# Four engines in order of emission in a two-layer attention, with deferred work and a later plan for the output projections

## The chip, the cores and the metric

The kernel runs on one core of a Trainium2 chip. The core has five engines with a queue each: TensorE (PE in the profile, its weight loads as PEld), VectorE (DVE), ScalarE (ACT), GpSimd (POOL) and SyncE (SP), which here only issues transfers. The metric is the device time of one execution in microseconds (us), smaller being better.

## What is computed

The reference applies the same two blocks twice, attention A and then a gated MLP B, to 2048 rows of 640 numbers. Cut to what matters:

```python
def A(x):                                  # 32 heads of 20, 4 segments of 512 rows
    q, k, v = x @ wq, x @ wk, x @ wv       # by head
    M = z = 0
    for s in range(4):
        logits = qs @ ks.T * scale + causal_mask
        a_dot = softmax(logits) @ vs
        pq = phi(qs)                       # phi(t) = t + 1 if t > 0 else exp(t)
        a_mem = (pq @ M) / (pq @ z + 1e-6)
        outs += [g * a_mem + (1 - g) * a_dot]
        M, z = M + phi(ks).T @ vs, z + sum(phi(ks))
    return concat(outs) @ wo

def B(x):
    z = gelu(x @ w_in)                     # halves z1, z2 of 864
    gate = w_sp @ layernorm(z2) + b_sp     # 2048 x 2048, over the rows
    return (z1 * gate) @ w_out

for layer in range(2):
    x = x + A(layernorm(x))
    x = x + B(layernorm(x))
```

Products are made in float16 halves: a number is split into a high part and the rest (`..h`, `..l`), and a product is three matmuls, high by high, high by low and low by high.

## The kernel before

Each layer has three phases. Phase 1a is the attention, phase 1b the remaining output projections and the first product of B, phase 2 the product with `w_sp` and the second product. The change is in phase 1a (and in two helpers that it calls).

**Steps.** The heads of a segment are taken in 16 pairs, so there are 64 pairs in a layer. A pair is scored in 3 steps, 192 in all, 48 in a segment. In a step (`scores`, L713) PE makes a part of two products: `es`, the logits of pair n with keys on partitions, and `mp`, those of pair n + 2 with queries on partitions, for the row maxima. Each has one bank pair of PSUM. ACT then takes the exponential of `es` into `P` (L747), and DVE reduces `mp` to `mx` (L754: 1024 columns in the first step of three, 768 and 256 in the second, 512 in the third). The finished maxima of a pair are transposed by PE (`maxes`, L773, `mtp`), split by ACT and DVE into `mr` (L775, L776), and written by SP into four rows of the query tile `qs`, so that the next score product subtracts them. `cast` (L764, L765) splits `P` into `PH` on ACT and `PL` on POOL. `pvs` (L795) is the product with the values, `combine` (L799) divides (`rs`, `ab` on DVE), adds on POOL, and after the last pair of a group of heads (a unit, five in a segment) splits the result `oat` into `ohl` and stores it.

**Dense work between steps.** The rest of the attention's products are spread between the steps. `unit` (L600) makes the queries and keys of a unit of heads: 15 matmuls each into `qps` and `kps`, the split into `qhl` and `khl` (L217, L218), and the feature map phi: `eq` (an exponential on ACT, L621, and a product on DVE, L622), then `phq` or `phk` on DVE (L624). Keys are split again into `phl` (L629, L630) and transposed by a transfer into `pkh`, `pkl` (L633). `update` (L666) adds a unit's phi(k) by v to the memory: PE into `mup` (L676, L678), DVE into `mst` (L680). `read` (L637) reads the memory: PE into `num`, DVE `den` and `gm` (L660 to L663). `value` (L551) makes the values of 128 rows in two products `vps`, evicted by ACT and DVE into `vs` (L567, L568). `project` (L578) makes the output projection of 128 rows in two products `yps`, added to the input by DVE (L592, L596); `load_o` (L571) fetches its input ahead of time. `prep` (L540) loads, normalises, splits and transposes 128 rows of input for the products; `split_t` (L202) has the cast `xnhl` (L205). All dense products share two PSUM banks (tag `dn`); `mtp`, `mup` and a part of `num` share one (tag `ms`).

**What sets the order.** `phase1a` (L943) puts PE alone under a hand-written order (`manual_schedule`): PE's instructions stand as the code emits them, step by step. The instructions of the other engines are put in order by the framework's scheduler, from its own estimate of the times. `run` (L825) emits: before step 0, `early` makes the first four blocks of values and the first unit; then in each step the fetch of a pair, its scores, the maxima, the value products, the casts, and up to the step's end what four streams have due: `fills` (loads of inputs ahead of their use), `background` (weights of the next phases: reductions for their scales, L52 and L58, and splits), `dense`, and `reads`. The dense stream follows `plan` (L857), one string for a segment: a digit is a unit of that segment (0 the first one of the next), `v` a block of values and `p` an output projection. Each string is spread evenly over 48 steps, LEAD = 14 steps ahead of the segment. 12 of the 16 projections (`NWO`) are made here; phase 1b does the last four. Phase 1b also splits the first half of `w_in` (`wi0h`, L72, and `wi0l`, L73); the scheduler is free to put such instructions of ACT, DVE and POOL among those of the attention, where buffers allow.

```python
        ctx.enter_context(g.tc.manual_schedule(engines={mybir.EngineType.PE}))
        ...
        plan = ["1v2v3v4v0", "1234vvvv0pp", "1p2p3v4vv0vp", "1p2p3p4pppp"]
```

Of the kernel before, what the change touches and what calls it, by code (L numbers as in the profile page):

```python
# [8 lines left out]
F32 = mybir.dt.float32  # L9
F32R = mybir.dt.float32r  # L10
F16 = mybir.dt.float16
# [64 lines left out]
class Weight:  # L76
# [12 lines left out]
    def load(self, stage, width=864, tag="wst"):  # L89
# [4 lines left out]
        if self.made:  # L94
            for t, d in ((self.h, self.kept[0]), (self.l, self.kept[1])):
                nc.sync.dma_start(t[:, :full], d[:, :full])
                if rest:
                    nc.sync.dma_start(t[:rest, full], d[:rest, full])
                yield
            return  # L100
        for k in range(self.nk):
            n = 128 if k < full else rest
            for c in range(0, self.cols, width):
# [3 lines left out]
                split_scaled(self.g, self.h[:n, k, c:c + w], self.l[:n, k, c:c + w], st, self.c)  # L107
                yield
        for t, d in ((self.h, self.kept[0]), (self.l, self.kept[1])):
# [57 lines left out]
def other_scales(g, stage, pool, psum, tag):  # L167

    nc = g.nc
    for i, w in enumerate((g.wo, *g.wi, g.wu)):  # L170
        width = D if w.cols == D else w.cols // 2
        j = 0
        for k in range(w.nk):
            n = min(128, w.dram.shape[0] - 128 * k)
            for c in range(0, w.cols, width):
                t = stage.tile([128, D], F32, tag="bg", name="wmst")[:n, :width]
                nc.sync.dma_start(t, w.dram[k * 128:k * 128 + n, w.c0 + c:w.c0 + c + width])
                nc.vector.tensor_reduce(g.wap[:n, i, j:j + 1], t, AX.X, ALU.max, apply_absolute_value=True)
                j += 1
                yield  # L180
# [6 lines left out]
def layernorm(g, xt, out, d, nch, mult=1.0):  # L187
# [11 lines left out]
    nc.vector.tensor_scalar(out, xt, mv[:, 0:1], rs, ALU.subtract, ALU.mult)  # L199
# [290 lines left out]

class Attention:
# [9 lines left out]
    def __init__(self, g, x, o_d, x1_d):  # L501
# [7 lines left out]
        self.mem, self.last = None, -1  # L509
# [30 lines left out]
    def prep(self, t):  # L540
        g, nc = self.g, self.nc
# [3 lines left out]
        xn = self.e1.tile([128, D], F32, tag="xn", name="xn")  # L545
        layernorm(g, xt, xn, D, 2, XS)
        xh, xl = self.xt[s % 2]
        hl = self.e1.tile([128, 2, D], F16, tag="xh", name="xnhl")
        split_t(g, hl[:, 0], hl[:, 1], xh[:, :, c], xl[:, :, c], xn, low=nc.gpsimd)

    def value(self, t):  # L551
# [4 lines left out]
        for n in range(2):  # L556
# [8 lines left out]
            v = self.vs[s % 2][:, t % 4, n * 16:(n + 1) * 16, :]  # L565
            ps = ps.rearrange("p (h d) -> p h d", d=DH)
            nc.scalar.mul(v[:, :, 0:DH], ps, QS)  # L567
            nc.vector.scalar_tensor_tensor(v[:, :, DH + 1:], ps, QS, v[:, :, 0:DH], ALU.mult, ALU.subtract)  # L568
# [9 lines left out]
    def project(self, t):  # L578
# [7 lines left out]
        for n in range(2):  # L586
# [9 lines left out]
            nc.vector.scalar_tensor_tensor(x1[:, c], ps, g.yw, xt[:, c], ALU.mult, ALU.add)  # L596
        nc.sync.dma_start(self.x1_d[t], x1)


    def unit(self, s, m):  # L600
# [3 lines left out]
        for nm in ("q", "k"):  # L604
            if nm == "k" and self.mem is not None:
                yield from self.update(*self.mem)
# [9 lines left out]
            hl = self.u2.tile([128, 2, L], F16, tag="hl", name=f"{nm}hl")  # L616
            split_psum(g, hl[:, 0], hl[:, 1], ps, QS)
            self.stack(nm, s, m, hl)
            if (nm == "q" and s > 0) or (nm == "k" and s < NSEG - 1):
                e = self.u2.tile([128, L], F32, tag="tmp", name="eq")  # L620
                nc.scalar.activation(e, ps, AF.Exp, scale=g.rq if nm == "q" else g.rk)  # L621
                nc.vector.tensor_scalar(e, e, 1.0, g.gq if nm == "q" else g.gk, ALU.min, ALU.mult)  # L622
                ph = (self.u4 if nm == "q" else self.u1).tile([128, L], F32, tag=f"ph{nm}", name=f"ph{nm}")
                nc.vector.scalar_tensor_tensor(ph, ps, 0.0, e, ALU.max, ALU.add)  # L624
                if nm == "q":
                    self.phq[m] = ph
                else:
                    hl = self.u2.tile([128, 2, L], F16, tag="hl", name="phl")
                    nc.scalar.mul(hl[:, 0], ph, g.sig)  # L629
                    nc.vector.scalar_tensor_tensor(hl[:, 1], ph, g.sig, hl[:, 0], ALU.mult, ALU.subtract)  # L630
                    self.pk = [self.u1.tile([128, 4, 128], F16, tag="pk" + p, name="pk" + p) for p in "hl"]
                    for i, o in enumerate(self.pk):
                        nc.sync.dma_start(o, hl[:, i], transpose=True)  # L633
        if s < NSEG - 1:
            self.mem = (s, m)

    def read(self, s, m):  # L637
# [7 lines left out]
        for c0 in range(0, nh, 6):  # L645
# [3 lines left out]
            p, tag = (self.pm, "ms") if c0 else (self.pd, "dn")  # L649
            tp = p.tile([128, L], F32, tag=tag, name="num")[:, :4 * n * (DH + 1)].rearrange("p (t h d) -> p t h d", t=4, h=n)  # L650
            for t in range(4):
# [3 lines left out]
                if low:  # L655
# [3 lines left out]
            den = self.u2.tile([128, 4, 6], F32, tag="den", name="den")[:, :, :n]  # L659
            nc.vector.scalar_tensor_tensor(den, tp[:, :, :, DH], g.epsd, g.gate[:, heads[c0]:heads[c0] + n].unsqueeze(1).to_broadcast((128, 4, n)),  # L660
                                           ALU.add, ALU.mult)
            nc.vector.reciprocal(den, den)
            nc.vector.tensor_tensor(gm[:, :, c0:c0 + n, :], tp[:, :, :, 0:DH],  # L663
                                    den.unsqueeze(3).to_broadcast((128, 4, n, DH)), ALU.mult)

    def update(self, s, m):  # L666

        g, nc = self.g, self.nc
        self.mem = None
# [10 lines left out]
        nc.vector.tensor_tensor(new, mp, g.bmask[:, m, :n].unsqueeze(2).to_broadcast((128, n, DH + 1)), ALU.mult)  # L680
        if s > 0:
            nc.gpsimd.tensor_tensor(new, new, old, ALU.add)
# [327 lines left out]
```

## Time and profile before

| | us |
|---|---|
| median of 3 runs | 2587.47 |
| lowest and highest of them | 2585.75, 2590.23 |
| the profiled execution | 2581.99 |
| its span | 2580.3 |
| first layer: attention from the first value product to the last value product by P | 31.9 to 752.6 |
| second layer: the same | 1318 to 2007.8 |

Over the span the engines are busy as follows (us, share of the span, instructions):

```profile
PE 2276.9 (88%) x21706; PEld 1360.2 (53%) x21706; DVE 1505.0 (58%) x2806; ACT 1154.7 (45%) x1398; POOL 899.5 (35%) x713
```

Two kinds of numbers are used below. A view by stretches gives, for a window of time, the busy time of each engine, the clock that TensorE was granted in it (PEclk, 1.00 is full speed) and the share of time in which the DMA engines worked. A row of waits reads "engine, tile and line that waited <- engine, tile and line that it waited for: total us, times, longest us".

### The profile page before, as it was taken

To read this page: it belongs to the slowest core of one execution; us is meant where nothing else is said; L and a number is where in the kernel's file an instruction comes from. 1 tells how busy PE (TensorE), PEld (TensorE's weight loads), DVE (VectorE), ACT (ScalarE), POOL (GpSimd) and SP (SyncE) were. 2 spreads that over 40 slices of the span, in tenths; PEclk is the share of its full clock that TensorE was granted. 3 is DMA by queue.
4 is the path that set the end of the run, shared out by engine and by line. 5 is a ranking of instruction groups with operands and counts; after the bars stand their busy time and mean duration, and the time that the engine had idled before them with its cause. 6 is when DMAs were issued, how large, how long until landed. Compare 5 with 4: busy or idle time off the path is not lost.

```text
span 2580.3 us, 53929 instructions
## 1 busy us (share of the span) xinstructions
PE 2276.9 (88%) x21706; PEld 1360.2 (53%) x21706; DVE 1505.0 (58%) x2806; ACT 1154.7 (45%) x1398; POOL 899.5 (35%) x713
## 2 busy tenths in 40 slices
PE   4688788899779998999988888888997999999998
PEld 2354455565545554555554545555654555555555
DVE  8677776767754454544335777776775554454432
ACT  4366666677643232211124766756775332121110
POOL 2166566677631000000022656666775110000000
PEclk9899799899879999999999989989997999999999
DMA  6643444534443488767643334344343435776663
GB/s 188 178 92 92 127 132 106 116 84 115 126 112 96 100 223 215 185 145 158 143 102 81 91 86 100 94 110 95 101 116 109 96 89 134 206 187 152 156 138 70
DMA packets 522187, 325.27 MB, mean 126 GB/s; under 512 B 423056, under 2 KB 468240, under 8 KB 516816
## 3 DMA queue, kind: packets, MB, share of 16 engines
q1 hardware_dynamic: 521936, 321.82, 51.0%
q8 instruction: 170, 2.79, 0.5%
q14 instruction: 81, 0.66, 0.1%
HBM read 148.26 MB, written 85.34 MB: 91 GB/s over the span
## 4 chain that ended last, share of the span: by engine, by line
PE 51%; DVE 11%; DMA 10%; ACT 6%; issue 4%; SPq 3%; POOL 3%; ACTq 0%; DVEq 0%; POOLq 0%
PE gp L365 16%; PE zp L283 12%; PE cyp L394 6%; DMA wr<-in_B_w_sp_dram 3%; DVE mx L754 3%; PE pv L795 2%; PE qps L613 2%; PE es L738 2%; PE kps L613 2%; PE vps L561 2%; ACT PH L764 2%; POOL PL L765 2%; ACT P L747 2%; PE yps L592 2%; PE mp L738 2%
## 5 line engine op out<-in xcount | busy, mean ns | idle before, releaser
L765 POOL TENSOR_TENSOR PL<-P,PH 128x1280 f16<-128x1280 f32 x248 | 649.8, 2621 | 379.7 <-ACT PH L764 361.7
L754 DVE TENSOR_REDUCE mx<-mp 128x2 f32<-128x1024 f32 (+3 forms) x512 | 409.0, 819 | 160.0 <-PE mp L710 158.3
L747 ACT ACTIVATE P<-es,sc 128x1024 f32<-128x1024 f32 (+1 forms) x384 | 372.2, 969 | 278.6 <-PE mp L710 226.4
L764 ACT CAST PH<-P 128x1280 f16<-128x1280 f32 x256 | 319.2, 1248 | 7.9 <-PE pv L795 1.7
L365 PEld LDWEIGHTS <-wth 128*128 128x128 f16 x2048 | 200.3, 98 | 180.2 <-DMA wth<-wnh 9.3
L365 PE MATMUL gp<-zh,wth 128*128 128x432 f16 x1024 | 271.0, 346 | 8.4 <-DMA wth<-wnh 8.4
L365 PE MATMUL gp<-zh,wtl 128*128 128x432 f16 x1024 | 270.6, 346 | 1.0 <-DMA wtl<-wnl 0.9
L365 PE MATMUL gp<-zl,wth 128*128 128x432 f16 x1024 | 271.0, 346 | 0.0
L738 PE MATMUL es<-qs,kb 64*128 64x512 f16 (+3 forms) x1024 | 147.6, 318 | 76.5 <-ACT P L747 66.1
L368 ACT ACTIVATE u<-gp,bsp,un 128x864 f32<-128x864 f32 x32 | 34.2, 1069 | 386.3 <-PE gp L365 384.7
L198 POOL TENSOR_TENSOR lnrs<-lnve,mhalf 128x1 f32<-128x1 f32 x96 | 58.5, 618 | 410.7 <-DVE lnve L197 386.0
L738 PE MATMUL mp<-kb,qs 60*128 60x512 f16 (+3 forms) x1024 | 144.2, 314 | 62.6 <-DVE mx L754 61.3
L381 POOL MEMSET unh<- 128x32 f16 x32 | 4.0, 125 | 559.1 <-DMA uh<-unh 507.4
L283 PEld LDWEIGHTS <-th 128*128 128x128 f16 x1280 | 125.6, 99 | 112.2 <-issue 3.4
L341 DVE TENSOR_REDUCE am<-wr 128x1 f32<-128x2048 f32 x32 | 73.2, 2286 | 172.8 <-DMA wr<-in_B_w_sp_dram 172.8
L795 PE MATMUL pv<-vs,PH 128*128 128x41 f16 x2560 | 170.6, 184 | 2.4 <-DVE ab L811 2.4
L795 PE MATMUL pv<-vs,PL 128*128 128x41 f16 x2560 | 167.9, 183 | 5.4 <-POOL PL L765 4.4
L710 PEld LDWEIGHTS <-big 64*128 64x128 f16 x4096 | 140.5, 98 | 43.8 <-issue 8.6
L795 PEld LDWEIGHTS <-PH 128*128 128x128 f16 x2560 | 151.0, 98 | 13.2 <-ACT PH L764 2.6
L738 PEld LDWEIGHTS <-kb 64*128 64x128 f16 x1024 | 46.9, 94 | 208.2 <-issue 193.6
L795 PEld LDWEIGHTS <-PL 128*128 128x128 f16 x2560 | 147.4, 98 | 7.9 <-POOL PL L765 4.7
L351 ACT ACTIVATE wnh<-wr,ivw 128x1024 f16<-128x1024 f32 x64 | 72.0, 1145 | 177.9 <-DVE ivw L346 106.3
(196 smaller groups left out, 4843.3 us busy)
## 6 DMA issues: line engine op xcount, KB each, us to landing
wr<-in_B_w_sp_dram SPq DMA_DIRECT2D x32, 1024.0 KB
x<-x SPq DMA_DIRECT2D x56, 320.0 KB
qs<-stq SPq DMA_DIRECT2D x256, 60.0 KB
kb<-stk SPq DMA_DIRECT2D x256, 60.0 KB
z<-z SPq DMA_DIRECT2D x32, 432.0 KB
cz<-z SPq DMA_DIRECT2D x32, 432.0 KB
xt<-in_A_x_dram SPq DMA_DIRECT2D x32, 320.0 KB
stq<-qhl SPq DMA_DIRECT2D x40, 256.0 KB
```

The costliest lines, as they stand in the source:

```text
L283: nc.tensor.matmul(zp[:, n, :FHH], a[:, k, :], b[:, k, c:c + FHH], start=(k == 0 and j == 0), stop=(k == KD - 1 and j == 2))
L341: nc.vector.tensor_reduce(am, wr, AX.X, ALU.max, apply_absolute_value=True)
L365: nc.tensor.matmul(gp[:, n, :FHH], a[:, k, :], b[:, k, n * FHH:(n + 1) * FHH], start=(k == 0 and j == 0), stop=(k == NT - 1 and j == 2))
L394: nc.tensor.matmul(yp[:, n, :320], a[:kn[k], k, :], b[:kn[k], k, n * 320:(n + 1) * 320], start=(k == 0 and j == 0), stop=(k == KO - 1 and ...
L613: nc.tensor.matmul(ps, a[:, k, c], b[:, k, :], start=(i == 0), stop=(i == 14))
L710: nc.tensor.matmul(out[:, o + c.start:o + c.stop], g.big[r, 64 - 64 * s:192 - 64 * s], g.mask[nm][r, m], start=False, stop=s == 1, skip_gr ...
L738: nc.tensor.matmul(out[:, h, o:o + w], a[r, ac], b[r, bc], start=o == 0, stop=False, skip_group_check=True)
L747: nc.scalar.activation(P[:, :, 512 * c:512 * c + ew], es[:, :, :ew], AF.Exp, scale=g.esc)
L754: nc.vector.tensor_reduce(self.mx[m][:, :, i], mp[:, :, o:o + w], AX.X, ALU.max)
L764: nc.scalar.copy(PH, P[:, h])
L765: (nc.gpsimd if h == 0 or n < self.N - self.TAIL else nc.vector).tensor_tensor(PL, P[:, h], PH, ALU.subtract)
L795: nc.tensor.matmul(pv[:, i, h, :], x[:, c:c + 128], v[:, j, h0 + h, :], start=(j == 0 and x is PH), stop=(j == i and x is PL), skip_group_ ...
```

## The change

Four engines, and not PE alone, keep the order of emission in the attention; SP stays with the scheduler. So the code now emits each piece of work at the step at which its engine is meant to do it. `post(k, f)` puts a function on a list that is run k steps later, right behind that step's scores; with a third argument it waits for a step with that remainder by 3.

```diff
+ENGINES = {mybir.EngineType.PE, mybir.EngineType.Activation, mybir.EngineType.DVE, mybir.EngineType.Pool}
...
+    def post(self, k, f, c=None):
+        if self.now is None:
+            f()
+            return
+        t = self.now + max(k, 1)
+        while c is not None and t % 3 != c:
+            t += 1
+        self.later.setdefault(t, []).append(f)
...
-        ctx.enter_context(g.tc.manual_schedule(engines={mybir.EngineType.PE}))
+        ctx.enter_context(g.tc.manual_schedule(engines=ENGINES))
```

In `run`, the maxima of a finished pair go ahead of the step's scores, the posted work behind them, and the last projections are spread over the rest of the attention (69 steps, END = 200). LEAD is 15 and not 14:

```diff
+        END = 3 * N + self.LV + 3
...
-        plan = ["1v2v3v4v0", "1234vvvv0pp", "1p2p3v4vv0vp", "1p2p3p4pppp"]
+        plan = ["1v2v3v4v0", "1234vvvv0p", "1p234vvvv0", "1p2p34pppppppp"]
...
+            span = G if s < nseg - 1 else END - 2 - G * s + LEAD
...
-                beg = G * s - LEAD + G * acc / tot
+                beg = G * s - LEAD + span * acc / tot
...
-                    ev.append((beg - 6, 0, t))
+                    ev.append((beg - 11, 0, t))
...
-                    ev.append((beg - 5, 1, t))
+                    ev.append((beg - 3.5, 1, t))
...
-        for t in range(-3 * self.LM - self.LF, 3 * N + self.LV + 3):
+        for t in range(-LEAD, END):
+            self.now = t
...
-            self.scores(n, c)
             if c == 0 and 0 <= n - 1 + self.LM < N:
                 self.maxes(n - 1 + self.LM)
+            self.scores(n, c)
+            for f in self.later.pop(t, ()):
+                f()
```

The matmuls of dense work stay where the plan has them; what reads their results is posted. The split and feature map of queries and keys (`out`, cut here to its order) come a step later, with the exponential ahead of DVE's part of the split, and the keys' second split one step more; the memory update of a unit comes at a step that begins a pair, its eviction a step behind:

```diff
-                yield from self.update(*self.mem)
+                self.post(0, lambda mem=self.mem: self.update(*mem), 0)
+                self.mem = None
+                yield 840
...
+        def parts():
...
+            nc.scalar.mul(hl[:, 0], ps, QS)
+            if feature:
...
+                nc.scalar.activation(e, ps, AF.Exp, scale=g.rq if q else g.rk)
+            nc.vector.scalar_tensor_tensor(hl[:, 1], ps, QS, hl[:, 0], ALU.mult, ALU.subtract)
+            self.stack(nm, s, m, hl)
...
+            nc.vector.tensor_scalar(e, e, 1.0, g.gq if q else g.gk, ALU.min, ALU.mult)
...
+            nc.vector.scalar_tensor_tensor(ph[0], ps, 0.0, e, ALU.max, ALU.add)
...
+                self.post(1, keys)
...
+        self.post(1, parts)
```

In the same way `value`, `project`, `update` and the last part of `read` post their evictions by one step, `combine` posts the split `ohl` by two, and `prep` its statistics by three steps behind the load and its normalisation by five. The normalised input is written over the loaded one (`xt`, no `xn`). `num` always takes the bank of `mtp` (tag `ms`); before, its first part took one of the dense banks. `early` takes two blocks of input at a time. The weights that `background` loads are split, or reduced, when the next one's load has been issued, and its times are 6 + 1.2 i for the reductions and 55 + 1.3 (6 j + i) for the loads.

What the new order is shows in the program's rows. First DVE in the second layer's attention, near step 48, where a unit's queries are evicted while a memory update is due. Before:

```order
L754 TENSOR_REDUCE mx<-mp 128x2
L806 TENSOR_TENSOR rs<-pv,iomg 128x8
L776 SCALAR_TENSOR_TENSOR mr<-mtp,mr 8x128
L807 RECIPROCAL rs<-rs 128x8
L811 TENSOR_TENSOR ab<-pv,rs 128x328
L680 TENSOR_TENSOR mst_17174<-mup,bmask 128x147
L218 SCALAR_TENSOR_TENSOR qhl<-qps,qhl 128x512
L754 TENSOR_REDUCE mx<-mp 128x2 x2
L622 TENSOR_SCALAR eq<-eq,sc 128x512
L624 SCALAR_TENSOR_TENSOR phq<-qps,eq 128x512
```

And of the change:

```order
L830 TENSOR_REDUCE mx<-mp 128x2
L694 SCALAR_TENSOR_TENSOR phl<-phk,sc,phl 128x512
L852 SCALAR_TENSOR_TENSOR mr<-mtp,mr 8x128
L830 TENSOR_REDUCE mx<-mp 128x2
L679 SCALAR_TENSOR_TENSOR qhl<-qps,qhl 128x512
L683 TENSOR_SCALAR eq<-eq,sc 128x512
L685 SCALAR_TENSOR_TENSOR phq<-qps,eq 128x512
L830 TENSOR_REDUCE mx<-mp 128x2 x2
L752 TENSOR_TENSOR mst_17158<-mup,bmask 128x147
L882 TENSOR_TENSOR rs<-pv,iomg 128x8
L883 RECIPROCAL rs<-rs 128x8
L887 TENSOR_TENSOR ab<-pv,rs 128x328
```

The maxima's second half `mr` moved ahead of the reduction of its step and stands behind `phl` of the step before; the update's eviction `mst` moved a step behind the queries' three operations.

Second, ACT at the start of the first layer's attention, where `qs` is initialised, the inputs are cast (`xnhl`) and the first values are evicted (`vs`). Before:

```order
L537 ACTIVATE qs_351<-zinit,qrow 128x512
L567 ACTIVATE vs_357<-vps 128x16x20 x2
L205 CAST xnhl<-xn 128x640
L567 ACTIVATE vs_357<-vps 128x16x20
L205 CAST xnhl<-xn 128x640
L567 ACTIVATE vs_357<-vps 128x16x20 x2
L205 CAST xnhl<-xn 128x640
```

And of the change:

```order
L566 ACTIVATE qs_350<-zinit,qrow 128x512
L566 ACTIVATE qs_351<-zinit,qrow 128x512
L220 CAST xnhl<-xt 128x640 x2
L604 ACTIVATE vs_357<-vps 128x16x20 x8
L675 ACTIVATE qhl<-qps 128x512
```

Two casts that stood between evictions of values now stand ahead of all of them; the other two come before the initialisation.

Third, PE near the end of the first layer's attention, behind the value products that follow the 62nd of the 64 transpositions of maxima. Before:

```order
L795 LDWEIGHTS PL
L795 MATMUL pv<-vs_358,PL 128x41
L738 LDWEIGHTS kb_352
L738 MATMUL es<-qs_347,kb_352 128x384
L738 LDWEIGHTS kb_352
L738 MATMUL es<-qs_347,kb_352 128x384
```

And of the change:

```order
L871 LDWEIGHTS PL
L871 MATMUL pv<-vs_358,PL 128x41
L631 LDWEIGHTS o
L631 MATMUL yps<-woh,o 128x320
L631 LDWEIGHTS o
L631 MATMUL yps<-wol,o 128x320
L631 LDWEIGHTS o
```

A projection's matmuls stand between two steps where the next step's scores followed at once. In the same place of ACT's order the splits `wi0h` stood between exponentials; they come behind the last `ohl` of the layer now.

More of the change, by code (lines that the diff above doesn't have):

```diff
@@ L615, in unit @@
                     yield 216
[L616 to L633, printed above, removed]
```

150 lines of the change are left out of this document (106 added, 44 removed).

## The prediction

> **What bounds the kernel now.** The first view is the head of the profile page. The profiled execution took 2581.99 us, of which the span is 2580.3; the median of the runs shown is 2587.47, so 5.5 us above it. Sums are made against the profiled execution and the 5.5 is added at the end. A measurement of this kernel can tell about 0.2%, 5 us, from no change.
>
> ```profile
> span 2580.3 us, 53929 instructions
> ```
>
> The second view is the table by stretches, cut where one part of the attention ends: the first row of a layer is its start (the lead-in to step 0), the next five I call A, B, C, D and E.
>
> ```profile
> core 0: us, PE busy (x) PEld busy (x) DVE busy (x) ACT busy (x) POOL busy (x), PEclk, DMA share, GB/s
> 32.00:103.00 71.00, 50.88 (x300) 27.49 (x301) 45.34 (x100) 20.39 (x36) 12.81 (x14) 0.88 0.75 183
> 103.00:215.00 112.00, 90.67 (x1256) 53.18 (x1257) 82.43 (x143) 76.06 (x97) 64.36 (x34) 0.94 0.45 109
> 215.00:398.00 183.00, 146.78 (x1902) 91.90 (x1900) 134.21 (x235) 119.82 (x154) 107.95 (x69) 0.90 0.47 123
> 398.00:529.00 131.00, 109.89 (x1442) 70.30 (x1438) 90.48 (x174) 83.92 (x106) 85.66 (x61) 0.91 0.46 105
> 529.00:663.00 134.00, 125.06 (x1850) 80.20 (x1848) 95.67 (x184) 98.01 (x118) 100.09 (x66) 1.00 0.39 101
> 663.00:753.00 90.00, 61.57 (x892) 41.72 (x886) 56.05 (x95) 51.37 (x57) 49.49 (x34) 0.77 0.42 116
> 1318.00:1391.00 73.00, 54.63 (x344) 31.13 (x343) 29.57 (x63) 21.00 (x36) 11.38 (x13) 0.86 0.46 113
> 1391.00:1494.00 103.00, 87.48 (x1255) 51.64 (x1253) 77.28 (x130) 75.84 (x97) 64.33 (x34) 0.97 0.34 82
> 1494.00:1659.00 165.00, 139.93 (x1908) 89.25 (x1905) 121.12 (x211) 110.87 (x139) 106.91 (x69) 0.94 0.39 94
> 1659.00:1789.00 130.00, 108.67 (x1438) 69.84 (x1437) 90.55 (x174) 84.04 (x106) 85.69 (x61) 0.92 0.44 106
> 1789.00:1923.00 134.00, 124.85 (x1847) 80.09 (x1842) 95.64 (x184) 98.00 (x118) 99.89 (x66) 1.00 0.39 101
> 1923.00:2008.00 85.00, 61.48 (x884) 41.45 (x882) 50.61 (x89) 46.82 (x52) 48.73 (x34) 0.81 0.37 104
> ```
>
> The same stretches with line L747 alone count the steps, since each scoring step has one exponential (column: ACT busy, count).
>
> ```profile
> 103.00:215.00 112.00, 34.84 (x36) 0.94 0.45 109
> 215.00:398.00 183.00, 46.42 (x48) 0.90 0.47 123
> ...
> 663.00:753.00 90.00, 23.27 (x24) 0.77 0.42 116
> ```
>
> A holds 36 steps, B 48 and E 24; C and D hold the other 84 of a layer's 192 (36 and 48). In D every engine keeps up: PE is busy 125.06 of 134 us (0.93), the clock is granted in full, and a step takes 2.8 us. In B a step takes 3.8 and 3.4 us and in C 3.6, though no engine is nearer to full: these stretches end on waits between engines. The clock column adds that a part of PE's busy time is slow time. I take busy time times clock as PE's work at full clock. For A to E it is, in layer 1, 85.2, 132.1, 100.0, 125.1 and 47.4 us; in layer 2, 84.9, 131.5, 100.0, 124.9 and 49.8. Against the stretch lengths that is 0.74 of B and C together in layer 1 and 0.785 in layer 2, and 0.53 and 0.59 of E. What the attention can win is the distance of these shares from D's.
>
> The third view says what PE waits for (total, times, longest), here in B of layer 1:
>
> ```profile
> PE mup L676 <- DVE mr L776: 8.7, 4, 4.1
> PE es L738 <- ACT P L747: 8.3, 10, 2.3
> PE mp L738 <- DVE mx L754: 8.1, 8, 2.4
> PE wtp L52 <- DVE mr L776: 2.8, 1, 2.8
> ...
> PE es L738 <- DMA qs<-mr: 0.5, 2, 0.3
> ```
>
> None is a throughput limit. They are an eviction that came late because its engine did something else first: the memory update waits for the bank that the maxima hold, the scores for the exponential and the reductions. In the tail, 690 to 729 us, where PE has no dense work left to put between two steps:
>
> ```profile
> PE es L738 <- ACT P L747: 11.6, 5, 3.9
> PE mp L738 <- DVE mx L754: 8.7, 5, 3.2
> ```
>
> **The change, part by part.** No instruction is added or removed on the four engines, so every term is a wait or a displacement.
>
> *Three projections go from B and C to D and E.* One row of a view by line prices a projection: the line L592 over the first layer.
>
> ```profile
> 0.00:1300.00 1300.00, 58.27 (x360) 32.62 (x360) 0.94 0.55 136
> ```
>
> At 30 matmuls a tile these are 12 tiles, so 58.27/12 = 4.86 us each, 4.55 at full clock; three are 13.6 us. PE's work becomes 218.5 (layer 1) and 217.9 us (layer 2) in B and C together, 186.1 and 188.3 in D and E.
>
> *Order and deferral in B and C.* The waits above should shrink: the maximum's transposition and its two evictions come first in a step, and all evictions of dense work come at least a step behind their matmuls. The trace cannot show an in-order DVE. The bounds by the nearest rows: nothing won (0.74, 0.785), or a share like D's (0.93). Midway is 0.835 and 0.86. But DVE is loaded more here than in D: 134.21 + 90.48 = 225 us in layer 1, 212 in layer 2, which in 264 us would be 0.80 to 0.85, where D shows 0.71 (95.67 of 134). So I stay just under the middle and take 0.83: 218.5/0.83 = 263 and 217.9/0.83 = 262 us. Layer 1 has in B the splitting of weights and the scale chain (its B is 18 us longer than layer 2's, the wait on wtp is in it); I leave 10 of these. Sum: 273 for 314, **-41**; 262 for 295, **-33**.
>
> *A.* Same argument from shares of 0.76 and 0.82 towards 0.93: 0.88. Layer 2: 84.9/0.88 = 97 for 103, **-6**. Layer 1 carries 9 us more than layer 2 now (the reductions for the weight scales), which I leave: 106 for 112, **-6**.
>
> *D and E.* Dense work is spread over 69 steps and not 48, so PE has something between the last steps' scores. D falls from its 0.93 a little as the same work gets thinner, and the last steps drain; 0.90 is taken (bounds 0.77, today's 172.5/224, and 0.93). 186.1/0.90 = 207 for 224, **-17**; 188.3/0.90 = 209 for 219, **-10**. It costs nothing in phase 1b unless the twelfth projection ends later than the last step; then PE waits there as it does today.
>
> *The start of a layer.* The rows are two of ACT's timeline (start, duration), and PE's waits of layer 1's start (32 to 103 us, two rows) and layer 2's (1318 to 1391, two rows):
>
> ```profile
> 40.52 0.75 ACT L567 ACTIVATE vs<-vps 128x320 f16<-128x320 f32 x2
> 46.25 0.72 ACT L205 CAST xnhl<-xn 128x640 f16<-128x640 f32 x1 [2.04 <-DMA xtl<-xnhl]
> ```
>
> ```profile
> PE mup L676 <- DMA pkh<-phl: 6.8, 1, 6.8
> PE vps L561 <- DVE phk L624: 3.9, 1, 3.9
> ```
>
> ```profile
> PE vps L561 <- DVE vs L568: 10.1, 3, 8.5
> PE mup L676 <- DMA pkh<-phl: 3.9, 1, 3.9
> ```
>
> Now ACT evicts the first values at 40.5 us, between the casts of the inputs, and the last cast comes at 46.25. In the new order all four casts and the ten initialisations stand ahead of the first value eviction; PE fills its two dense banks and waits until about 47.5, so +7. Against it the two waits behind the first keys (6.8 and 3.9) are now a deferred update and should lose about half: -5. Layer 1 **+2**. In layer 2 the 8.5 us wait is of the kind that stays, since casts still come first; 2 of the 10.1 and 3 of the others go: **-5**. Bounds for each layer: +7 and -10.
>
> *Weight splitting behind the attention.* Five splits on ACT stand between exponentials of the tail now, and behind the last eviction in the new order:
>
> ```profile
> L72 ACT ACTIVATE wi0h<-wst,iv 128x864 f16<-128x864 f32 x5 | 5.1, 1014 | 5.6 <-DMA wst<-in_B_w_in_dram 5.6
> ```
>
> Phase 1b's first product needs the first of them; 5.1 us less the part that the last combinations cover, **+4** in layer 1 (layer 2 loads the kept halves).
>
> *Queues passed.* The loads of inputs are issued 11 steps ahead of the value product and not 6; the transposed loads for a projection 3.5 and not 5 steps ahead, about 10 us at 2.9 us a step. The order of issue on SP is still the scheduler's. I cost both at nothing; without that cover each of the ten late projections could wait for its load as layer 2's update does at the start (3.9 us, above); at half of that it is 20 us a layer, which is in the range.
>
> *DVE and POOL side by side.* Two operations of DVE that read SBUF vary widely in one shape in layer 2's attention (ns: min, median, max):
>
> ```profile
> L630 DVE SCALAR_TENSOR_TENSOR phl<-phk,sc,phl x15: 739/1887/2589, 1365.5 to 1772.4; 128x512 f16<-128x512 f32 x15
> L622 DVE TENSOR_SCALAR eq<-eq,sc x30: 435/487/2141, 1363.4 to 1905.2; 128x512 f32<-128x512 f32 x30
> ```
>
> These are spread by a factor of over three, as if another engine's work held something they need. If all came at their slowest, DVE had 15 x 0.70 + 30 x 1.65 = 60 us more a layer; if all at their fastest, 15 x 1.15 + 30 x 0.05 = 19 less. Order decides it and the trace can't say which way; I take no change and leave it to the range. [...]
>
> Sum: -12 -41 -33 -17 -10 +2 -5 +4 = -112. 2581.99 - 112 + 5.5 = **2476 us**. Its own range: shares in B and C between 0.78 and 0.88 move 34 us either way: 2440 to 2512.
>
> **The rivals.** (1) *All like D.* With 0.93 in A to E the terms are -11 -12 -69 -61 -24 -17, with the +1 of the start and the splits -193: **2395**. For it: no wait in the rows is a throughput limit. Against: DVE's load.
>
> (2) *Only the clock is won.* The idle time stays as long, but comes in shorter pieces, so PE runs at full clock: busy time times (1 - clock) is 44 us in layer 1 (5.4, 14.7, 9.9, 0, 14.2) and 31 in layer 2 (2.6, 8.4, 8.7, 0, 11.7); -75 + 1, **2513**. For it: D is the only stretch at 1.00, and it has the shortest waits. [...]
>
> (3) *The waits move to SP's queue.* What a step's maxima write back goes through SP (the last row of B's waits, 0.5 us now). If these get later as fast as the engines get earlier, B and C win nothing: -12 -27 + 1, **2549**. The 0.5 us speaks against it.
>
> (4) *Slower: DVE's strict order.* In a step with a key product DVE has two reductions, the key's split, eq, phk and a combination in a row:
>
> ```profile
> L754 DVE TENSOR_REDUCE mx<-mp 128x2 f32<-128x768 f32 x56 | 53.4, 954 | 7.5 <-PE mp L710 7.1
> L754 DVE TENSOR_REDUCE mx<-mp 128x2 f32<-128x256 f32 x56 | 23.3, 415 | 0.0
> L624 DVE SCALAR_TENSOR_TENSOR phk<-kps,eq 128x512 f32<-128x512 f32 x13 | 8.9, 685 | 0.2
> L811 DVE TENSOR_TENSOR ab<-pv,rs 128x328 f32<-128x328 f32 x54 | 27.0, 499 | 3.1
> ```
>
> That is 1.37 + 0.69 (the split is as large as phk) + 0.49 + 0.69 + 0.50 = 3.7 us, and phl's 1.9 follows in the next step, ahead of mr, on which PE's update, and through it PE's whole queue, now waits. The scores have one bank each for es and mp, so what is late on DVE stops PE a step later. DVE's work is 134.21/48 and 121.12/48, mean 2.66 us a step, PE's 2.6. With no overlap a step takes 5.26, with full overlap 2.66. If only 1.0 us overlaps, it takes 4.3: 84 steps are 361 us for 314 and 295, +113, less the other terms' 38: **2662**. It turns slower when a step takes more than (314 + 295)/168 + 38/168 = 3.86 us, so when less than 1.4 of 2.66 us overlap. Against: B shows 3.4 with an order that nobody wrote out.
>
> (5) *It does not do what it says.* Order may already be nearly that of emission, and waits trade places: 2587.
>
> **How the numbers follow.** Chances: forecast 0.46; like D 0.13; clock only 0.16; SP's queue 0.12; slower 0.09; no change 0.04. Faster by over 0.2% is the first four, 0.87. The range goes from 2400 to 2575: it leaves out the slower case and the lower half of "like D", 0.16 in all.
>
> **What would show it.** Right: a step of B and C at about 3.1 us with the wait of mup for mr gone; the clock of the tail near 1.0 and L592's successor between the last scores; the first value evictions after 47 us; the wi0 splits after the last pv. Wrong: DVE's rows for mr with idle time in front of them on PE's maximum transposition, PE's scores waiting for reductions longer than 2.4 us, or the qs<-mr wait growing from 0.5 us to tens.

## The result, and the profile after

The change makes the kernel slower: 2692.69 us median (2687.76 to 2700.92, 4 runs) against 2587.0 (2585.75 to 2590.23, 4 runs), a ratio of 1.041 with a 95% interval of 1.0382 to 1.0437. The profiled execution took 2692.43 us, its span is 2690.7.

The same cut as before, at steps 0, 36, 84, 120 and 168 and the last value product, here of the change (us, busy time of each engine with its count, granted clock, DMA share, GB/s):

```profile
core 0: us, PE busy (x) PEld busy (x) DVE busy (x) ACT busy (x) POOL busy (x), PEclk, DMA share, GB/s
...
103.00:217.00 114.00, 92.32 (x1272) 54.77 (x1268) 86.54 (x160) 77.97 (x98) 67.26 (x37) 0.93 0.49 133
217.00:425.00 208.00, 149.29 (x1863) 92.35 (x1864) 143.13 (x252) 118.55 (x152) 109.41 (x71) 0.84 0.45 117
425.00:566.00 141.00, 108.36 (x1431) 67.93 (x1428) 87.70 (x172) 83.62 (x107) 87.17 (x61) 0.88 0.40 90
566.00:706.00 140.00, 119.88 (x1753) 75.59 (x1751) 92.34 (x179) 97.77 (x119) 99.00 (x66) 0.96 0.30 82
706.00:792.00 86.00, 68.06 (x949) 46.65 (x946) 52.15 (x97) 47.43 (x52) 45.93 (x34) 0.88 0.46 115
...
1448.00:1557.00 109.00, 88.26 (x1275) 53.73 (x1274) 73.59 (x136) 77.68 (x99) 68.06 (x37) 0.97 0.36 88
1557.00:1739.00 182.00, 141.80 (x1856) 89.13 (x1856) 113.86 (x220) 109.22 (x137) 106.06 (x71) 0.88 0.32 80
1739.00:1880.00 141.00, 108.58 (x1434) 68.07 (x1431) 87.73 (x172) 83.78 (x107) 87.24 (x61) 0.88 0.37 90
1880.00:2020.00 140.00, 119.87 (x1752) 75.52 (x1749) 92.30 (x179) 97.60 (x119) 98.95 (x66) 0.96 0.31 82
2020.00:2107.00 87.00, 69.47 (x951) 47.02 (x946) 52.65 (x97) 47.53 (x52) 45.91 (x34) 0.86 0.56 139
```

B and C together went from 314 to 349 us in layer 1 and from 295 to 323 in layer 2; D went from 134 to 140 in both, and lost its full clock (1.00 before, 0.96 now). Only layer 1's E got shorter (90 to 86; layer 2's 85 to 87). No engine has more to do: DVE's busy time over the span fell from 1505.0 to 1482.5 us, and PE makes fewer matmuls in B (1863 for 1902 in layer 1). PE's busy time rose all the same, from 2276.9 to 2309.0 us, while it ran at a lower clock (in that B 146.78 us at 0.90 became 149.29 at 0.84). So of the 110 us that the span grew, 78 are idle time of PE and 32 are longer busy time.

The rest of the loss lies behind the attention. From the last value product by P (`pv`) to the last product of phase 1b (`zp`) it took 185.8 and 184.1 us before and takes 201.1 and 194.6 now, 26 us more in all. Before, the first `zp` stood 24 and 25 us ahead of the last value product, between the last steps; now it comes 5.6 and 3.0 us behind it.

What PE waits for names one row, here B of layer 1 and the attention's end (706 to 792 us) of the change (total, times, longest):

```profile
PE pv L871 <- DVE ab L887: 23.4, 11, 6.1
PE mp L814 <- DVE mx L830: 8.5, 5, 2.6
PE num L716 <- DVE gm L729: 4.9, 1, 4.9
```

```profile
PE pv L871 <- DVE ab L887: 6.9, 7, 1.8
PE mp L814 <- DVE mx L830: 4.0, 3, 2.9
```

Over the whole execution it is the costliest wait. The rows before, three of them:

```profile
PE es L738 <- ACT P L747: 66.1, 63, 3.9
PE mp L738 <- DVE mx L754: 61.3, 57, 5.1
...
PE pv L795 <- DVE ab L811: 2.4, 2, 1.2
```

And the four longest of the change:

```profile
PE pv L871 <- DVE ab L887: 144.9, 93, 6.1
PE vps L599 <- DVE vs L605: 36.4, 10, 14.3
PE mp L814 <- DVE mx L830: 25.4, 34, 2.9
PE es L814 <- ACT P L823: 21.7, 43, 2.3
```

The scores' waits fell as forecast (mp from 61.3 to 25.4 us, es from 66.1 to 21.7). What came in their place is above all the value product waiting for `ab`, the division of the pair before, which frees the one `pv` bank; `num` and `mtp` now wait on DVE too (for `gm` and `rs`, 46 us in all). DVE's timeline shows why `ab` is late. It is the second step of a pair near step 97 of layer 2 (start, duration, instruction, idle before it):

```profile
1783.34 1.29 DVE L830 TENSOR_REDUCE mx<-mp 128x2 f32<-128x768 f32 x2 [2.37 <-PE mp L786]
1784.55 0.30 DVE L752 TENSOR_TENSOR mst<-mup,bmask 128x147 f32<-128x147 f32 x1
1785.49 0.69 DVE L679 SCALAR_TENSOR_TENSOR khl<-kps,khl 128x512 f16<-128x512 f32 x1 [0.64 <-ACT eq L678]
1786.10 0.48 DVE L683 TENSOR_SCALAR eq<-eq,sc 128x512 f32<-128x512 f32 x1
1786.61 0.69 DVE L685 SCALAR_TENSOR_TENSOR phk<-kps,eq 128x512 f32<-128x512 f32 x1
1787.21 0.15 DVE L882 TENSOR_TENSOR rs<-pv,iomg 128x8 f32<-128x8 f32 x1
1787.40 0.20 DVE L883 RECIPROCAL rs<-rs 128x8 f32<-128x8 f32 x1
1787.71 0.50 DVE L887 TENSOR_TENSOR ab<-pv,rs 128x328 f32<-128x328 f32 x1
...
1791.65 0.28 DVE L852 SCALAR_TENSOR_TENSOR mr<-mtp,mr 8x128 f16<-8x128 f32 x1 [2.19 <-ACT mr L851]
```

and PE at the same place:

```profile
1788.26 0.18 PE L871 MATMUL pv<-vs,PH 128*128 128x41 f16 x1 [3.12 <-DVE ab L887]
```

The division takes 0.9 us and its input is old: PE's products for it ended by 1781.1 us in the trace. DVE then sat idle for 2.37 us ahead of the reductions, waiting for PE's scores of this step, and could have divided. In its strict order it first reduces, then evicts the update and the keys, which were deferred to just this step, and only then divides. PE has done the next step's scores by then and stands at the next pair's first value product for 3.12 us; its scores, the transposition of the maxima and `mr` all move back by that, and DVE idles for 2.19 us ahead of `mr` in turn. Before, the scheduler had the division in the pair's first step, ahead of `eq` and `phk` (layer 2, near step 98):

```profile
1702.34 0.16 DVE L806 TENSOR_TENSOR rs<-pv,iomg 128x8 f32<-128x8 f32 x1
1702.52 0.28 DVE L776 SCALAR_TENSOR_TENSOR mr<-mtp,mr 8x128 f16<-8x128 f32 x1
1702.84 0.20 DVE L807 RECIPROCAL rs<-rs 128x8 f32<-128x8 f32 x1
1703.14 0.50 DVE L811 TENSOR_TENSOR ab<-pv,rs 128x328 f32<-128x328 f32 x1
1703.56 0.48 DVE L622 TENSOR_SCALAR eq<-eq,sc 128x512 f32<-128x512 f32 x1
```

### The profile page after: what moved, and what is told of

Read it like the earlier page. It is cut to its first block, busy times and chain, and to the rows that moved or that the text cites. A ratio compares the mean times of both kernels' runs of the same rounds, so it can differ in the third digit from the quotient of the medians.

```text
span 2690.7 us, 53982 instructions
## 1 busy us (share of the span) xinstructions
PE 2309.0 (86%) x21706; PEld 1374.4 (51%) x21706; DVE 1482.5 (55%) x2806; ACT 1155.3 (43%) x1398; POOL 897.1 (33%) x713
## 5 line engine op out<-in xcount | busy, mean ns | idle before, releaser
L871 PE MATMUL pv<-vs,PH 128*128 128x41 f16 x2560 | 172.8, 186 | 145.2 <-DVE ab L887 144.9
L208 POOL TENSOR_TENSOR lnrs<-lnve,mhalf 128x1 f32<-128x1 f32 x96 | 66.2, 697 | 480.2 <-DVE lnve L207 472.9
L814 PE MATMUL mp<-kb,qs 60*128 60x512 f16 (+3 forms) x1024 | 143.0, 314 | 25.6 <-DVE mx L830 25.4
L814 PE MATMUL es<-qs,kb 64*128 64x512 f16 (+3 forms) x1024 | 145.1, 318 | 23.0 <-ACT P L823 21.7
L380 PEld LDWEIGHTS <-wtl 128*128 128x128 f16 x1024 | 100.0, 98 | 88.2 <-DMA wtl<-wnl 1.9
```

What stands on the lines that cost most here:

```text
L380: nc.tensor.matmul(gp[:, n, :FHH], a[:, k, :], b[:, k, n * FHH:(n + 1) * FHH], start=(k == 0 and j == 0), stop=(k == NT - 1 and j == 2))
L814: nc.tensor.matmul(out[:, h, o:o + w], a[r, ac], b[r, bc], start=o == 0, stop=False, skip_group_check=True)
L871: nc.tensor.matmul(pv[:, i, h, :], x[:, c:c + 128], v[:, j, h0 + h, :], start=(j == 0 and x is PH), stop=(j == i and x is PL), skip_group_ ...
```

## The experiments

Each ratio is to the kernel before, in the runs of the same chip, with its 95% interval; 1% is 26 us.

**The division ahead of the step's scores.** In the changed kernel:

```diff
+            p, r = divmod(t - self.LV - 2, 3)
+            if r == 0 and 0 <= p < N:
+                self.combine(p, *pairs[p])
             self.scores(n, c)
...
-            p, r = divmod(t - self.LV - 2, 3)
-            if r == 0 and 0 <= p < N:
-                self.combine(p, *pairs[p])
             until(t + 1)
```

> The changed kernel with one move: the division of a pair (rs, ab, and the additions on GpSimd) is emitted ahead of its step's scores, not at the step's end behind the reductions and the deferred evictions. Theory (the one pv bank is released too late, because ab stands behind other work in DVE's strict order): PE's wait of pv for ab falls from 145 us to under 40, and the time from 2693 to 2580-2620 us. Rival (DVE in strict order is late wherever ab stands): the wait moves to reductions or mr, time 2660 or more.

2643.05 us, 1.0235 (1.0218 to 1.0252): 1.75 points, 45 us, come back with this one move. The wait for `ab` falls from 144.9 to 7.4 us. Others grew, `mp` from 25.4 us and `mtp` from 0.6:

```profile
PE mp L814 <- DVE mx L830: 67.7, 79, 3.7
PE mtp L849 <- DVE mx L830: 41.8, 21, 4.3
```

So both expectations were half right: the place of the division cost 45 us, less than the 70 to 110 expected, and a third of the wait's own 145. The rest of that wait came back as others.

**Which engine's order.** The changed kernel with `ENGINES` cut to TensorE, and to all but VectorE:

```diff
-ENGINES = {mybir.EngineType.PE, mybir.EngineType.Activation, mybir.EngineType.DVE, mybir.EngineType.Pool}
+ENGINES = {mybir.EngineType.PE}
```

> The changed kernel with TensorE alone in order of emission, as before; deferral by steps, the new plan and the spread of the projections stay. Theory (strict order of the other engines costs, not the plan): pv's wait for ab is under 10 us and the time 2540-2610 us. Rival (the moved projections and deferred matmuls cost): 2650 or more.

> The changed kernel with VectorE's order left to the scheduler; TensorE, ScalarE and GpSimd stay in order of emission. Theory (it is VectorE's order): near the run with TensorE alone, 2550-2620 us, pv's wait for ab under 15 us. Rival (ScalarE's order sets the pace): 2660 or more.

TensorE alone: 2614.05 us, 1.0125 (1.0109 to 1.014). All but VectorE: 2619.6 us, 1.0146 (1.0131 to 1.0161), no clear difference between the two. VectorE's strict order is thus the step from 1.0146 to 1.041, 2.6 points or 68 us, and the division's place is 45 of them; the other 23 stay open. In the starts of the layers VectorE's order helps: from the first product that makes values to the first exponential's scores it takes 86.9 and 81.5 us with VectorE free and 71.2 and 77.9 in the change, so in the steps the order costs more than the 68. But both runs stay above the kernel before: something in the code costs time with the other engines free.

**The plan.** The changed kernel with the strings and the 48 steps of before; and the other way, the kernel before with the new strings and the spread:

```diff
-        plan = ["1v2v3v4v0", "1234vvvv0pp", "1p2p3v4vv0vp", "1p2p3p4pppp"]
+        plan = ["1v2v3v4v0", "1234vvvv0p", "1p234vvvv0", "1p2p34pppppppp"]
...
+            span = G if s < nseg - 1 else END - 2 - G * s + LEAD
```

> The changed kernel with the plan of before (seven projections in the last segment, over 48 steps). Theory (the plan is not the cause): 2680-2710 us, and the last scores wait more. Rival (the later projections push phase 1b back and cost the 25 us that it takes longer): 2660-2670 us.

> The kernel before with the new plan and the spread of the last projections, nothing else. Theory (the plan takes work out of the stretches that wait and fills the tail, for more than the 20-25 us that phase 1b loses): 2540-2570 us. Rival (phase 1b's loss eats the gain): 2578-2600 us.

The old plan in the changed kernel gave 2680.26 us, 1.0384 (1.0361 to 1.0406), not clearly below the change's 1.0382 to 1.0437: the attention got 10 and 4 us longer, and phase 1b 15 and 10 shorter. The new plan alone in the kernel before gave 2558.33 us, **0.9914** (0.988 to 0.9947): it is faster than both kernels, and no other run is clearly faster than it. Its D and E of both layers:

```profile
522.00:655.00 133.00, 119.95 (x1785) 75.89 (x1780) 95.04 (x181) 98.14 (x120) 100.08 (x66) 0.99 0.31 86
655.00:732.00 77.00, 63.78 (x948) 44.03 (x947) 52.55 (x98) 46.89 (x52) 50.40 (x34) 0.93 0.57 127
...
1766.00:1898.00 132.00, 120.37 (x1791) 76.11 (x1788) 95.30 (x182) 98.16 (x120) 100.52 (x66) 0.99 0.32 87
1898.00:1978.00 80.00, 64.03 (x948) 44.49 (x946) 50.63 (x98) 46.69 (x52) 50.22 (x34) 0.94 0.61 149
```

E is 13 and 5 us shorter, its clock 0.93 and 0.94 for 0.77 and 0.81. Phase 1b takes 196.2 and 194.4 us, 10 longer in each layer: the matmuls of its first product left the tail.

**The maxima's place, and both.** The transposition of the maxima and its evictions put back behind the scores, with and without the division's move:

```diff
-            if c == 0 and 0 <= n - 1 + self.LM < N:
-                self.maxes(n - 1 + self.LM)
             self.scores(n, c)
+            if c == 0 and 0 <= n - 1 + self.LM < N:
+                self.maxes(n - 1 + self.LM)
```

> The maxima put back behind the scores, the division left at the step's end as in the change. Theory (the two places act apart): pv's wait for ab stays above 100 us, time 2650-2690 us. Rival (the maxima's place is also what makes ab late): pv's wait for ab under 60, time under 2640 us.

> The division ahead of the scores as in the first run, and the maxima (transposition mtp and its evictions mr) put back behind the step's scores. Theory (a transposition that stands first in its step has no slack to the reduction of the step before): mtp's wait for mx falls from 42 us to under 10, time from 2643 to 2600-2620 us. Rival (the maxima then reach the query tile too late): es waits for qs<-mr above 30 us in all, time 2640 or more.

Alone: 2733.35 us, 1.0578 (1.056 to 1.0596); pv's wait for `ab` stays, at 148.8 us, and the time lies above both expectations. With the division first: 2662.01 us, 1.0306 (1.0291 to 1.0322). Both are slower than without the move, by 1.7 and 0.7 points: in strict order the early maxima are right, and the theory that they cost was wrong. In the run with both, the waits only changed name, mtp for mx (41.8 us) into mup for mr (41.2).

> Division ahead of the scores, maxima behind them, and the plan of before. Theory (the plan's cost is the overlap of the attention's end with phase 1b, independent of order): 10 to 20 us under the run with both moves and the new plan, phase 1b's first product again over 20 us ahead of the last value product. Rival (in a faster attention the late projections pay): equal or slower than that run.

2663.86 us, 1.0321 (1.0294 to 1.0349): the plan makes no difference to the time there. Phase 1b is 16 and 11 us shorter, as the theory said, and the attention longer by as much or more.

**Two other orders in a step.** With the division first, the transposition between the `es` and the `mp` products; or all deferred work ahead of the scores.

```diff
+        mid = c == 0 and 0 <= n - 1 + self.LM < self.N
...
+            if mid and x == "q":
+                self.maxes(n - 1 + self.LM)
+                mid = False
             for h in range(2):
```

> Division ahead of the scores as in the first run, and the transposition of the maxima between the step's es products and its mp products. Theory (es stands idle behind a transposition that waits for the reduction of the step before, which mp needs anyway): 2625-2638 us, and PE's wait of mtp for mx falls from 42 to under 25 us. Rival (the wait is that of the one mp bank, and only changes its name): 2639-2650 us.

```diff
+            for f in self.later.pop(t, ()):
+                f()
             self.scores(n, c)
-            for f in self.later.pop(t, ()):
-                f()
```

> Division ahead of the scores, and the deferred work of a step ahead of its scores too, not behind them. Theory (DVE waits for the scores, 67 us in layer 1, while evictions that are ready stand behind them): 2600-2630 us. Rival (what matters is how soon the reductions free mp; evictions ahead of them make PE wait more): 2660 or more.

The first: 2645.68 us, 1.0254 (1.0233 to 1.0274), no change in the time, as the rival said: mtp and mp wait for the same reduction. The wait of mtp for mx did fall, to 21.9 us, as the theory said, while es's wait for `P` rose from 18.5 to 30.9. The second: 2740.1 us, 1.0647 (1.058 to 1.0713). The evictions did not fit into DVE's idle time ahead of the reductions; standing there they made the one `mp` bank late (67.7 us of waits with the division first alone):

```profile
PE mp L814 <- DVE mx L830: 161.7, 112, 2.8
PE es L814 <- ACT P L823: 68.9, 63, 4.7
```

**What costs with the other engines free.** Between the new plan alone (0.9914) and TensorE alone by hand (1.0125) lie 2.1 points. First TensorE alone with the old plan:

> TensorE alone in order of emission, deferral by steps kept, the plan of before. Theory (of the 32 us that TensorE alone with the new plan loses, 20 are the plan): 2590-2600 us, phase 1b back to 184-186 us a layer; what is left over the kernel before (10-15 us) is the deferral and the maxima's place. Rival (deferral costs all of it): 2610-2618 us.

2658.91 us, 1.0297 (1.0277 to 1.0317). Both expectations missed: with this order of TensorE the new plan gains 45 us, where it gained 22 in the kernel before. Then the maxima first in the kernel before:

> The kernel before, TensorE's order alone by hand, with one move: a pair's maxima ahead of the step's scores. Theory (this move is most of what TensorE's new order costs with the other engines free): 2600-2625 us, mtp waiting for mx 30 us or more. Rival (the move is harmless, as in strict order): 2575-2592 us.

2581.02 us, 0.9996 (0.9982 to 1.001): harmless there. Then `num`'s bank, the update a step after it is posted, and both, in the changed kernel with TensorE alone:

```diff
-            tp = self.pm.tile([128, L], F32, tag="ms", name="num")
+            p, tag = (self.pm, "ms") if c0 else (self.pd, "dn")
+            tp = p.tile([128, L], F32, tag=tag, name="num")
...
-                self.post(0, lambda mem=self.mem: self.update(*mem), 0)
+                self.post(0, lambda mem=self.mem: self.update(*mem))
```

> TensorE alone in order of emission with the new code (2614 us), and the first part of num back in a dense bank. Theory (one bank for mtp, mup and all of num makes TensorE's queue wait): 2590-2605 us, mup's and num's waits on DVE fall from 58 us to under 35. Rival (the dense banks are as scarce): 2608 or more.

> TensorE alone in order of emission with the new code, and the memory update a step after it is posted, not at the next step that begins a pair. Theory (at a pair's first step the update comes right behind the transposition, whose bank it needs, so TensorE waits for mr): mup's wait for mr falls from 45 us to under 20 and the time to 2585-2600 us. Rival (the wait is hidden elsewhere): 2608 or more.

> Both of these. Theory (both act, by different waits): 2570-2590 us. Rival (what is left is the deferral of the evictions, which no place of the update mends): 2600 or more.

2623.84 us, 1.0159 (1.0137 to 1.0181); 2610.45, 1.0116 (1.0088 to 1.0144); 2610.83, 1.0107 (1.0087 to 1.0126). None of them brings the time clearly down. Nor did they remove the wait of mup for mr (45.2 us with TensorE alone; 54.6, 37.6 and 46.4 in these three), so they do not clear the bank as a cause. Last, no deferral of evictions, and then none at all with the maxima behind the scores (`if True:` in `post`):

```diff
-        if self.now is None:
+        if self.now is None or c is None:
             f()
```

> TensorE alone in order of emission with the new code, and every deferred eviction emitted at once as before (the memory updates alone stay deferred). Theory (with the other engines free, it is the later place of the evictions in the code, which the scheduler follows, that costs most of the 56 us between the new plan alone and TensorE alone by hand): 2555-2580 us. Rival (it is the rest of TensorE's new order: update, num, LEAD, the earlier maxima): 2600 or more.

> TensorE alone in order of emission with the new code, no deferral at all (memory updates inline too) and the maxima behind the scores, as before; LEAD 15, the step of the reads, num's bank and the loads' and weights' new times stay. Theory (maxima first together with deferred updates is most of the 46 us left over the new plan alone): 2555-2575 us. Rival (it is the numbers that stay: LEAD, reads, loads, weights): 2590 or more.

2604.72 us, 1.0091 (1.0064 to 1.0119), and 2563.84 us, 0.9933 (0.9914 to 0.9953). The second is close to the plan alone, so the new numbers (LEAD, reads, loads, weights) cost nothing clear, and the maxima ahead of the scores with the deferred updates cost 1.6 points, 41 us, under the new plan with free engines. The rows of the first,

```profile
PE mp L814 <- DVE mx L830: 97.9, 76, 4.7
PE mup L746 <- DVE mr L852: 49.0, 20, 5.3
PE es L814 <- ACT P L823: 41.6, 61, 2.6
PE mtp L849 <- DVE mx L830: 24.9, 17, 2.9
```

and of the second,

```profile
PE mp L814 <- DVE mx L830: 87.6, 73, 6.5
PE es L814 <- ACT P L823: 50.0, 71, 3.7
PE mup L746 <- DMA pkh<-phl: 20.4, 6, 6.8
...
PE mup L746 <- DVE mr L852: 12.5, 8, 3.1
```

differ in the two that the bank of the maxima sets: mup for mr 49.0 and 12.5, mtp for mx 24.9 and not among the shown. Which of the two moves it is was not separated; the maxima alone cost nothing under the old plan, and freeing the update from a pair's first step gained nothing by itself.

**The division's place without strict order.**

> The kernel before with the new plan (2558 us), and the division emitted ahead of the scores; DVE's order is the scheduler's. Theory (the scheduler already puts the division as early as the value product allows, so its place in the code tells only in strict order): 2552-2566 us. Rival (the division's place matters to the scheduler too): under 2545 us.

2559.4 us, 0.9915 (0.9896 to 0.9935), as the plan alone: the place in the code tells only where it is also the engine's order.

The path from the kernel before to the change, in points of its time:

| | ratio | step |
|---|---|---|
| new plan alone | 0.9914 | -0.9 |
| and the new numbers | 0.9933 | not clear |
| and maxima first, updates deferred | 1.0091 | +1.6 |
| and evictions deferred | 1.0125 | intervals overlap |
| and ScalarE, GpSimd in strict order | 1.0146 | intervals overlap |
| and VectorE: the change | 1.041 | +2.6 |
| from there, the division first | 1.0235 | -1.75 |

The steps hold in this sequence; other sequences share them out differently, as the plan and the maxima showed.

## Why the prediction was wrong

It said 2476 us; 2693 was measured, above its range. The step that failed is *Order and deferral in B and C*: -41 and -33 us, on the assumption that the waits there only shrink and that PE's share of full-clock work rises to 0.83. Measured are 349 and 323 us, +35 and +28; that is 137 of the 217 us by which the forecast is off. What the runs showed in its place is a new wait: VectorE's strict order made the division late, PE waited 144.9 us for the one `pv` bank, and the division's move gave back 45 us of the 68 that VectorE's order costs. The prediction took the waits of before as an order to be mended, and priced the new order by D, where DVE has less to do: the waits it named did shrink (mp, es, mup for mr), but it never asked what the combination's place does to PE. Its row for the slower rival even had the chain "two reductions, the key's split, eq, phk and a combination in a row", and then looked behind it, to phl and mr, and not at the end of that very row, where one `pv` bank hands the delay to PE. Busy time times clock gives 149.29 x 0.84 + 108.36 x 0.88 = 221 of 349 us in layer 1, 220 of 323 in layer 2: shares of 0.63 and 0.68, under those of before.

**The rivals.** The fourth, at 0.09, came in kind: DVE's strict order, with 4.15 and 3.85 us a step in B and C, where it priced 4.3 and a turn at 3.86. Its path was another: it had phl and mr delay PE's update, and late reductions hold the scores' banks, and these waits fell. That its total, 2662, is only 31 us short is luck: B and C cost 63 us where it had 113, and the other terms, which were to give 38 back, cost 47. "All like D", "only the clock" and "SP's queue" did not come; the clock in B even fell, from 0.90 and 0.94 to 0.84 and 0.88, and es's wait for the maxima's transfer fell from 10.1 us to 0.4. That shorter pieces of idle time bring the full clock was the author's estimate, and the trace before does not show it: A of layer 2 was granted 0.97 with no wait of PE above 1.7 us, and D of layer 2 was granted 1.00 with one of 1.8. The range also left out the case of no change, at 2587, so 0.195 of its chances lay outside it and not 0.16.

**A, and D and E.** A was to get 6 us shorter in each layer and got 2 and 6 longer, with 13.0 and 12.6 us of waits for `ab`. D and E were to be 207 and 209 us; the change has 226 and 227. The plan alone has 133 + 77 = 210 and 132 + 80 = 212, so the term came out, but partly by luck: PE's work there is 178 and 179 us at full clock, not 186 and 188, at a share of 0.85, not 0.90. The trace shows two projections, not three, leaving B and C (120 matmuls of `yps` before, 60 after, 30 to a projection), and 60 matmuls of `zp` leave E. In the change, 16 and 18 us of waits for `ab` in D and E took the gain back (D's step rose though its work fell). "It costs nothing in phase 1b" was wrong by about 10 us a layer: the first `zp` filled the tail before, and the projections only took its place. The 5.0 points (128 us) from the plan alone to the change lie in the rest of the bundle.

**The start.** Layer 1, +2, was about right: from the first product that makes values to the first exponential's scores it takes 71.1 us before and 71.2 after. The wait for the value evictions (`vs`), which now stand behind all four casts, grew from 3.2 to 14.3 us, and the two waits behind the first keys fell from 10.7 to 3.6. Layer 2 was to gain 5 and lost 5 (72.9 to 77.9): the wait for `vs` grew from 10.1 to 13.4 us and that for `pkh` from 3.9 to 4.8. *Weight splitting*, +4, seems to lie in phase 1b of layer 1, whose 15 us exceed layer 2's 10 by 5. But with VectorE free and ScalarE in order the splits stand behind the last value product too (768.5 us against 761.1), and phase 1b takes 196.5 us, as with the plan alone (196.2). The 5 us come only with VectorE's order: 199.7 to 202.0 us in every run that has it and the new plan.

**DVE and POOL side by side.** Left at no change in a range of -19 to +60 a layer; measured is a gain of VectorE's time, 16 us in layer 1 and 19 in layer 2 for the two operations together. In layer 2 of the change (ns: min, median, max):

```profile
L694 DVE SCALAR_TENSOR_TENSOR phl<-phk,sc,phl x15: 739/751/1425, 1421.5 to 1855.6; 128x512 f16<-128x512 f32 x15
L683 DVE TENSOR_SCALAR eq<-eq,sc x30: 475/477/597, 1419.4 to 2005.6; 128x512 f32<-128x512 f32 x30
```

The medians were 1887 and 487, the longest 2589 and 2141. In the trace before, all nine `phl` of layer 2 that took over 1 us (1.67 to 2.59) began while a subtraction of GpSimd (`PL`, 2.62 us in the median) was under way, and each ended 0.54 to 0.55 us after it; none of the six short ones (0.74 to 0.75 us) began in one. In the change 2 of 15 `phl` and 1 of 30 `eq` began in a subtraction, where before it were 9 and 11. With TensorE alone in order it is 7 and 18, with all but VectorE 2 and 4, so most of it comes with the order of ScalarE and GpSimd. The time did not profit: the attention got longer all the same.

## What to carry to other kernels

When an engine goes from a scheduler's order to a strict one, go through every single-buffered tile it releases and ask what stands ahead of the release in its queue; the small operation that frees a bank belongs ahead of work that waits for others. A wait of 145 us in a trace need not be worth 145 us: removing it gave 45 here, and other waits grew. Try the parts of a bundle alone: here one of them (the plan) was a gain of 0.9% that the rest hid.

## What was not expected of the hardware

In layer 2 `phl` took 0.75 us in the median where it had taken 1.89, and `eq` never more than 0.60 where it had reached 2.14, with the same shapes and operands; before, 9 of 15 and 11 of 30 began inside one of GpSimd's 2.6 us subtractions, and in the change 2 and 1. Each `phl` of layer 2 that began inside a subtraction, nine before and two in the change, lasted until 0.54 to 0.55 us after that subtraction's end, whether it had begun 0.5 or 2.0 us ahead of that end.
